# A fused attention and feed-forward kernel on one core: alternating K and Q transposes, finer loads for batch 0, a halved last tile, and paired scores from batch 1

## The chip, the core and the metric

The kernel runs on one core of a Trainium2 chip. The metric is the device time of one execution in microseconds (us), taken outside the profiler. The span in a profile is about 1.7 us shorter, because it begins at the first profiled instruction. Engines are named as in the profile: PE is the matrix engine (TensorE), PEld its weight loads, DVE VectorE, ACT ScalarE, POOL GpSimd, SP the engine that issues most DMAs, with q added for a sequencer.

Before the change the median was 360.2 us (359.94 to 360.87, 4 runs).

## The reference

Eight batches of gated attention (8 heads, 576 positions, head size 64) feed a gated feed-forward layer (width 512, hidden 1536).

```python
scores = q @ k.T / 8                                    # per batch and head
bias   = -(cum[:, None] - cum[None, :])                 # cum = cumsum(max(s, 0))
attn   = softmax(where(causal, -1e9, scores + minimum(bias, 0)))
x      = (attn @ v), heads joined                       # 4608 x 512
xn     = x / sqrt(mean(x * x) + 1e-6) * rms_g
out    = (silu(xn @ w_gate) * (xn @ w_val)) @ w_out     # 4608 x 512, float32
```

## The kernel before

The kernel records all operations with estimated durations. A list scheduler then fixes the order on each engine, and each operation is emitted in that order. `R.after(a, b)` is only an order for that scheduler. On the chip it holds where both stand on the same engine; between two engines only data dependencies make one wait.

The output tokens are worked off in nine chunks of 512. For each chunk, PE does the gate and value products (FFN1), then the output product (FFN2). The attention of the next batch is woven in between. The attention of batch 0 has to come first, and so it stands alone at the start.

These parts matter here (cuts are marked):

```python
def prep_transpose(b, which, hp, key, eng):             # K or Q of one head pair
    ...
    mms(0.6, [(t[64*j:64*j+64, c, :], raw[b][p0:p0+KP, 2*hp+j, c, :], ident_bf[...],
               c == 0, c == KC-1, True) for c in range(KC) for j in range(2)], key=key)
    ...                                                 # evicted by DVE (K) or ACT (Q)

def decay(key):                                         # DVE: max, then a scan of 64 x 576
    I("dve", "tensor_scalar", ..., out=s_all, in0=s_all, scalar1=0.0, op0=ALU.max)
    I("dve", "tensor_tensor_scan", ..., out=cum, data0=ones[...], data1=s_all, ...)
    ...

def att_out(b, tb, key):                                # scale a tile of rows, transpose it
    ...
    I("act", "activation", 0.5, out=x, in_=x, func=AF.Copy, scale=al[b % 2][:, 1, tb:tb+1])
    ...

def ffn2(c, key, step):                                 # O: 128 tokens x 512
    for tb in range(4):
        ...                                             # 12 matmuls of 512 columns
        I("act", "activation", 0.6, out=o, in_=O, func=AF.Copy, scale=0.5)
        I("sp", "dma_start", ..., out=out[t0+tb*128 : t0+(tb+1)*128, :], in_=o)

NTWO = 2                                                # paired scores from this batch on
WL = (0, 6, 12)                                         # gate and value weights in two pieces
...
for i in range(2):
    for w in range(2):
        load_runs(0, w, 2*i, 2*i+2, -100+i)             # K, Q, two heads each
for w in range(2):
    load_runs(0, w, 4, 8, -98)                          # K, Q, the other four heads
ident(ident_bf, -97)                                    # identity for the transposes, on POOL
ident(ident_F, -96)
load_rows(v_nat[0], v, 0, "pool", -94)
...
R.after(vops[2], norms[3])                              # v products of batch 0 on DVE
for o in wl[2:]:
    R.after(o, masks[0, HP-1])                          # second half of the weights
```

Of the kernel before, what the change touches and what calls it, by code (L numbers as in the profile page):

```python
# [75 lines left out]
class Plan:  # L76
# [58 lines left out]

    def schedule(self):
# [15 lines left out]
        def ready(o):  # L152
            t = 0.0
            for p, raw in o.preds.items():
                q = ops[p]
                if q.eng == o.eng and not q.dma:
                    t = max(t, q.done if raw and o.eng != "pe" else q.start)
                else:
                    t = max(t, q.done + self.HOP)
            return t  # L160
# [88 lines left out]
def kernel(  # L249
# [41 lines left out]
    NTWO = 2  # L291
# [138 lines left out]
    def prep_transpose(b, which, hp, key, eng):  # L430
        p0, dst = KP * which, (KT, QT)[which]
        t = lay(small_bank(), bf16, "p (c t) -> p c t", n=S, c=KC)
        mms(0.6, [(t[64 * j : 64 * j + 64, c, :], raw[b][p0 : p0 + KP, 2 * hp + j, c, :],
                   ident_bf[p0 : p0 + KP, p0 : p0 + KP],
                   c == 0, c == KC - 1, True) for c in range(KC) for j in range(2)], key=key)
        o = dst[b % 2][:, hp, 0:S].rearrange("p (t c) -> p t c", c=KC)
        i = t.rearrange("p c t -> p t c")
        if eng == "dve":
            I("dve", "tensor_copy", 0.68, key=key, out=o, in_=i)
        else:  # L440
            I("act", "activation", 0.57, key=key, out=o, in_=i, func=AF.Copy)
# [98 lines left out]
    masks = {}  # L540

    def unit_scores(b, us, keys, Es, cap):
# [11 lines left out]
        o = mms(0.1 + 0.32 * len(us), items, key=keys[0])  # L554
        for u, key in zip(us, keys):
            e = Es[u] = nxt("E", E)
            for j in range(2):
                I("act", "activation", 0.5, key=key, out=e[:, j], in_=banks_[u][j], func=AF.Exp,
                  scale=0.125)
            diag = e.rearrange("p j (c n) -> p (j c) n", n=128)[:, 0:8:2, :]  # L560
            masks[b, u] = I("pool", "affine_select", 0.59, key=key, out=diag, in_=diag,
              pattern=[[0, 4], [1, 128]], compare_op=ALU.is_ge, fill=0.0, base=0,
              channel_multiplier=-1)
            if u >= HP:
                last = e[:, :, 448:512]
                I("pool", "affine_select", 0.28, key=key, out=last, in_=last,
                  pattern=[[0, 2], [1, 64]], compare_op=ALU.is_ge, fill=0.0, base=0,
                  channel_multiplier=-1)
        return o

    def unit_av(b, u, key, Es):
# [10 lines left out]
        mms(0.2 if hf == 0 else 0.4,  # L582
# [20 lines left out]
    def att_alpha(b, t0, t1, key):  # L603
# [3 lines left out]
        I("pool", "tensor_tensor", 0.94, key=key, out=y, in0=m, in1=mhalf[:, 0 : t1 - t0],  # L607
          op=ALU.pow)

    def att_out(b, tb, key):  # L610
        x = x_blk[b % 2][:, tb, :]
        if b >= NPE:
# [7 lines left out]
        I("act", "activation", 0.5, key=key, out=x, in_=x, func=AF.Copy,  # L620
          scale=al[b % 2][:, 1, tb : tb + 1])
        p0 = 64 if tb == 4 else 0
        X = lay(small_bank(), bf16, "p (c t) -> p c t", n=DM, c=CC)
        mms(0.24, [(X[:, cc, :], x_blk[b % 2][:, tb, cc * 128 : (cc + 1) * 128], ident_bf,
# [6 lines left out]
    def attention(b, key, step, cap):  # L631
# [8 lines left out]
        for hf in range(2):  # L640
# [6 lines left out]
            att_alpha(b, tbs[0], tbs[-1] + 1, k2)  # L647
# [24 lines left out]
    def ffn2(c, key, step):  # L672
        t0 = c * DM
        for tb in range(4):
            O = bank("ffn", 6)
            for f in range(0, FB, 2):
                mms(0.432, [(O, Hs[:, fb, tb * 128 : (tb + 1) * 128], wout_sb[:, fb, :],
                             fb == 0, fb == FB - 1, False) for fb in (f, f + 1)],
                    key=key + step * (tb * FB + f))
            o = nxt("osb", osb)  # L680
            I("act", "activation", 0.6, key=key + step * (tb * FB + FB), out=o, in_=O,
              func=AF.Copy, scale=0.5)
            I("sp", "dma_start", 0.62, key=key, dma=0.75,
              out=out[t0 + tb * 128 : t0 + (tb + 1) * 128, :], in_=o)
# [3 lines left out]
    WL = (0, 6, 12)  # L688
# [11 lines left out]
    for i in range(2):  # L700
        for w in range(2):
            load_runs(0, w, 2 * i, 2 * i + 2, -100 + i)
# [4 lines left out]
    for w in range(2):  # L707
        load_runs(0, w, 4, 8, -98)
    ident(ident_bf, -97)
    ident(ident_F, -96)  # L710
    load_rows(v_nat[0], v, 0, "pool", -94)
# [11 lines left out]
    for hp in range(HP):  # L723
        prep_transpose(0, 0, hp, -80 + hp, "dve")
        prep_transpose(0, 1, hp, -80 + hp, "act")
# [6 lines left out]
    R.after(vops[2], norms[3])  # L732
    for o in wl[2:]:
        R.after(o, masks[0, HP - 1])
    raw_norm(0, 20)
    for w in range(2):
        for h in (0, 4):
            R.after(load_runs(1, w, h, h + 4, -45), masks[0, 2 * HP - 1])
    load_rows(v_nat[1 % len(v_nat)], v, 1, "pool", -44)
    for i in range(2):  # L740
        load_w(2, 6 * i, 6 * i + 6, -40)
    gl = I("sp", "dma_start", 0.5, key=30, dma=2.0, out=gB,
           in_=moe_rms_g.unsqueeze(0).to_broadcast([128, DM]))
    for c in range(NCH):
# [5 lines left out]
        if b < B:  # L750
            if b < NRUN:
                for hp in range(HP):
                    prep_transpose(b, 0, hp, K + hp, "dve")
                    prep_transpose(b, 1, hp, K + hp, "act")
            else:
                prep_cast(b, K - 14)
# [193 lines left out]
```

## Time and profile before

| What | Value | View |
|---|---|---|
| time | 360.2 us | timed runs |
| PE busy | 339.0 of 358.9 us | page, part 1 |
| first FFN1 matmul | 25.2 us | timeline |
| last PE work, end of span | 352.8, 358.9 us | timeline |

The page's part 1 gives busy microseconds, the share of the span and the instructions. Part 4 gives the shares of the chain that ended last.

```profile
PE 339.0 (94%) x2934; PEld 206.7 (58%) x2934; DVE 247.0 (69%) x486; ACT 231.6 (65%) x469; POOL 126.5 (35%) x211
...
PE 78%; DMA 9%; POOL 6%; DVE 3%; issue 1%; ACT 1%; DVEq 0%; POOLq 0%; ACTq 0%
```

PE is the bound. The run is the time until the first FFN1 matmul, plus the PE work after it, plus a tail. The next fence is the list of what PE waited for (what waited, what released it, total us, times, longest).

```profile
PE psa L376 <- POOL ident_bf masks.py:199: 5.8, 1, 5.8
PE psd L378 <- DVE vwa L361: 2.5, 1, 2.5
...
PE pse L376 <- ACT x_blka L361: 0.5, 1, 0.5
PE psg L376 <- ACT x_blka L361: 0.4, 1, 0.4
...
PE psh L376 <- ACT x_blka L361: 0.2, 1, 0.2
```

The first wait is for the identity. The 2.5 us are attention-times-V products (AV) of the second half of batch 0, which need a v product. The waits for `x_blka` are for scaled rows.

Next are PE's weight loads in batch 1, where PE is never idle. Each line with `k_nat` is one group of K or Q transposes.

```profile
38.54 0.65 PEld L376 LDWEIGHTS <-k_nat 64*64 64x64 bf16 x36 [0.21 <-issue]
...
40.20 0.55 PEld L376 LDWEIGHTS <-k_nat 64*64 64x64 bf16 x36 [0.21 <-issue]
...
41.77 0.36 PEld L376 LDWEIGHTS <-k_nat 64*64 64x64 bf16 x18 [0.21 <-issue]
```

A group of 18 that stands alone occupies PE for 0.40 us, counted from its start to the start of the next work. Two groups side by side take 0.69 and 0.59.

The tail, as the timeline and the list of DMA issues of that window have it (the last column of the issue is the time to landing):

```profile
352.92 0.60 ACT L361 ACTIVATE osbc<-psb 128x512 f32<-128x512 f32 x1 [2.04 <-PE psb L378]
353.54 0.33 SPq L361 DMA_DIRECT2D out_dram<-osbc  x1
```

```profile
out_dram<-osbc SPq DMA_DIRECT2D x1, 256.0 KB, 3.5
```

### The profile page before, as it was taken

To read this page: it belongs to the slowest core of one execution; us is meant where nothing else is said; L and a number is where in the kernel's file an instruction comes from. 1 tells how busy PE (TensorE), PEld (TensorE's weight loads), DVE (VectorE), ACT (ScalarE), POOL (GpSimd) and SP (SyncE) were. 2 spreads that over 40 slices of the span, in tenths; PEclk is the share of its full clock that TensorE was granted. 3 is DMA by queue.
4 is the path that set the end of the run, shared out by engine and by line. 5 is a ranking of instruction groups with operands and counts; after the bars stand their busy time and mean duration, and the time that the engine had idled before them with its cause. 6 is when DMAs were issued, how large, how long until landed. Compare 5 with 4: busy or idle time off the path is not lost.

```text
span 358.9 us, 7827 instructions
## 1 busy us (share of the span) xinstructions
PE 339.0 (94%) x2934; PEld 206.7 (58%) x2934; DVE 247.0 (69%) x486; ACT 231.6 (65%) x469; POOL 126.5 (35%) x211
## 2 busy tenths in 40 slices
PE   2969999999999999999999999999999999999993
PEld 2657776698668875888444554445445444444441
DVE  6586965798848992899467967995489538707820
ACT  3858998597678857877677568775876433233311
POOL 8987273301480375117502650357124100000000
PEclk9989999999999999999999999999999999999998
DMA  7999999999999899869978989995801150020011
GB/s 118 211 226 208 216 204 204 172 213 195 203 154 231 170 144 215 189 123 170 207 154 163 182 175 178 164 187 104 177 9 31 55 102 1 1 89 29 0 62 64
DMA packets 138357, 51.14 MB, mean 142 GB/s; under 512 B 127300, under 2 KB 132936, under 8 KB 138312
## 3 DMA queue, kind: packets, MB, share of 16 engines
q1 hardware_dynamic: 131688, 41.13, 60.9%
q0 software_dynamic: 6624, 9.44, 14.4%
q8 instruction: 25, 0.41, 0.5%
q14 instruction: 20, 0.16, 0.2%
HBM read 38.16 MB, written 9.44 MB: 133 GB/s over the span
## 4 chain that ended last, share of the span: by engine, by line
PE 78%; DMA 9%; POOL 6%; DVE 3%; issue 1%; ACT 1%; DVEq 0%; POOLq 0%; ACTq 0%
PE pse L378 12%; PE psa L378 10%; PE psh L378 10%; PE psb L378 10%; PE psf L378 9%; PE psd L378 9%; PE psc L378 9%; PE psg L378 8%; DMA wv_sb<-in_moe_w_val_dram 5%; DMA v_nata<-in_v_dram 4%; POOL v_nata L361 2%; POOL q_nat L361 1%; ACT sq_scr L361 1%; DVE Hs L361 1%; POOL Ee L361 1%
## 5 line engine op out<-in xcount | busy, mean ns | idle before, releaser
L378 PEld LDWEIGHTS <-wv_sb 128*128 128x128 bf16 x624 | 59.9, 98 | 32.9 <-issue 1.3
L378 PEld LDWEIGHTS <-wg_sb 128*128 128x128 bf16 x624 | 59.2, 98 | 30.7 <-issue 0.8
L378 PEld LDWEIGHTS <-Hs 128*128 128x128 bf16 x432 | 41.0, 98 | 45.6
L361 POOL TENSOR_SCALAR_AFFINE_SELECT Ea<-Ea 128x512 bf16<-128x512 bf16 x8 | 5.6, 699 | 61.6 <-ACT Ea L361 61.6
L361 POOL TENSOR_TENSOR vwb<-v_nata,wT 128x512 bf16<-128x512 f32 (+1 forms) x20 | 20.6, 1049 | 6.8 <-DMA v_nata<-in_v_dram 6.8
L378 PE MATMUL pse<-wout_sb,Hs 128*128 128x512 bf16 x96 | 22.5, 379 | 0.0
L378 PE MATMUL psf<-xnT,wv_sb 128*128 128x256 bf16 (+1 forms) x116 | 20.7, 313 | 0.0
L361 ACT ACTIVATE sq_scr<-x_blka 128x512 bf16<-128x512 bf16 x19 | 12.0, 630 | 12.0 <-DVE x_blka L361 11.6
L378 PE MATMUL psc<-xnT,wg_sb 128*128 128x256 bf16 (+1 forms) x104 | 18.8, 316 | 0.0
L361 DVE SCALAR_TENSOR_TENSOR x_blkb<-x_blkb,alb,gB 128x512 bf16<-128x512 bf16 x15 | 11.0, 779 | 10.8 <-POOL alb L361 10.7
L361 ACT ACTIVATE sq_scr<-x_blkb 128x512 bf16<-128x512 bf16 x20 | 12.6, 629 | 7.8 <-DVE x_blkb L361 7.3
L378 PE MATMUL psh<-wout_sb,Hs 128*128 128x512 bf16 x72 | 17.2, 379 | 0.0
L378 PE MATMUL psa<-wout_sb,Hs 128*128 128x512 bf16 x72 | 17.0, 379 | 0.0
L378 PE MATMUL psb<-xnT,wv_sb 128*128 128x256 bf16 (+1 forms) x100 | 16.5, 302 | 0.2 <-DVE u_sbc L361 0.2
L378 PE MATMUL psd<-xnT,wg_sb 128*128 128x256 bf16 (+1 forms) x88 | 16.5, 321 | 0.0
L361 ACT ACTIVATE sq_scr<-q_bf 128x1024 bf16<-128x1024 bf16 (+1 forms) x18 | 16.4, 912 | 0.1
L361 ACT ACTIVATE sq_scr<-k_bf 128x1024 bf16<-128x1024 bf16 (+1 forms) x18 | 16.3, 908 | 0.0
L361 DVE CAST q_bf<-q_nat 128x512 bf16<-128x512 f32 (+1 forms) x30 | 15.3, 510 | 0.9 <-ACT sq_scr L361 0.9
L378 PE MATMUL pse<-xnT,wg_sb 128*128 128x256 bf16 (+1 forms) x92 | 15.5, 305 | 0.0
L378 PE MATMUL psa<-xnT,wg_sb 128*128 128x256 bf16 (+1 forms) x84 | 15.5, 318 | 0.0
L361 POOL TENSOR_TENSOR vwa<-v_nata,wT 128x512 bf16<-128x512 f32 (+1 forms) x15 | 15.1, 1039 | 0.0
L361 DVE CAST k_bf<-k_nat 128x512 bf16<-128x512 f32 (+1 forms) x30 | 13.7, 456 | 0.0
(464 smaller groups left out, 850.4 us busy)
## 6 DMA issues: line engine op xcount, KB each, us to landing
v_nata<-in_v_dram SPq DMA_DIRECT2D x24, 256.0 KB, 5.3
k_nat<-in_k_dram SPq DMA_DIRECT2D x24, 256.0 KB, 3.6
q_nat<-in_q_dram SPq DMA_DIRECT2D x24, 256.0 KB, 4.5
out_dram<-osba SPq DMA_DIRECT2D x12, 256.0 KB, 2.4
out_dram<-osbb SPq DMA_DIRECT2D x12, 256.0 KB, 2.5
out_dram<-osbc SPq DMA_DIRECT2D x12, 256.0 KB, 2.4
v_nata<-in_v_dram POOLq DMA_DIRECT2D x8, 256.0 KB, 10.4
wg_sb<-in_moe_w_gate_dram POOLq DMA_DIRECT2D x2, 768.0 KB, 12.2
```

The source lines that it names most:

```text
L361: o = R.add(eng, us, lambda: f(**{n: real(a) for n, a in kw.items()}), outs, ins, key=key, lat=LAT[eng], kind=kind, dma=dma, name=outs[0]. ...
L378: nc.tensor.matmul(out, lhsT=lhsT, rhs=rhs, start=st, stop=sp)
```

## The change

The intent is to shorten the start (earlier identity, loads in finer pieces and in a fixed order, v products and one scaling moved), to let the K and Q transposes of a head pair share PE (they use different 64-row halves of it), to pay the cost of entering and leaving the scores less often in batch 1, and to shorten the last eviction and store. The durations that the scheduler assumes were also re-measured, which re-orders the later batches a little.

```diff
-    NTWO = 2
+    NTWO = 1
...
-    def prep_transpose(b, which, hp, key, eng):
-        p0, dst = KP * which, (KT, QT)[which]
-        t = lay(small_bank(), bf16, "p (c t) -> p c t", n=S, c=KC)
-        mms(0.6, [( ... ) for c in range(KC) for j in range(2)], key=key)
+    def prep_transpose(b, hp, key):
+        t = [lay(bank("kq", 4), bf16, "p (c t) -> p c t", n=S, c=KC) for w in range(2)]
+        mms(0.52, [( ... ) for c in range(KC) for j in range(2) for w in range(2)], key=key)
...
-        I("act", "activation", 0.5, key=key, out=x, in_=x, func=AF.Copy, scale=...)
+        if b == 0 and tb == 1:
+            I("dve", "tensor_scalar", 0.3, key=key, out=x, in0=x, scalar1=..., op0=ALU.mult)
+        else:
+            I("act", "activation", 0.72, key=key, out=x, in_=x, func=AF.Copy, scale=...)
...
+            nh = 2 if c == NCH - 1 and tb == 3 else 1       # ffn2: last tile in halves
+            ...                                             # matmuls, eviction, store per half
-    WL = (0, 6, 12)
+    WL = (0, 2, 6, 12)
...
-    for w in range(2):
-        load_runs(0, w, 4, 8, -98)
-    ident(ident_bf, -97)
+    loads += [load_runs(0, w, 2 * i, 2 * i + 2, -98) for i in (2, 3) for w in range(2)]
+    ident(ident_bf, -98.5)                                  # now before these four loads
...
-    R.after(vops[2], norms[3])
-    for o in wl[2:]:
+    for o in vops[2:]:
+        R.after(o, norms[3])
+    for o in loads[15:]:                                    # weights from the 2nd piece on
         R.after(o, masks[0, HP - 1])
+    for o in wl[4:]:                                        # 3rd piece
+        R.after(o, alphas[0, 0])
+    R.order(*loads)
```

Besides this, the masks and the power of batch 0's first half got priority on POOL, and batch 0's transposes of x got their own group of banks.

More of the change, by code (lines that the diff above doesn't have):

```diff
@@ L134, in after, with order @@
             o.preds.setdefault(p.n, False)
+    def order(self, *ops):
+        for p, o in zip(ops, ops[1:]):
+            o.preds.setdefault(p.n, None)
     def schedule(self):
@@ L155, in ready @@
                 q = ops[p]
-                if q.eng == o.eng and not q.dma:
+                if raw is None:
+                    t = max(t, q.start)
+                elif q.eng == o.eng and not q.dma:
                     t = max(t, q.done if raw and o.eng != "pe" else q.start)
@@ L427, in load_w @@
                  in_=src[:, lo:hi].rearrange("(cc p) f -> p cc f", p=128))
-    def prep_transpose(b, which, hp, key, eng):
-        p0, dst = KP * which, (KT, QT)[which]
-        t = lay(small_bank(), bf16, "p (c t) -> p c t", n=S, c=KC)
-        mms(0.6, [(t[64 * j : 64 * j + 64, c, :], raw[b][p0 : p0 + KP, 2 * hp + j, c, :],
-                   ident_bf[p0 : p0 + KP, p0 : p0 + KP],
-                   c == 0, c == KC - 1, True) for c in range(KC) for j in range(2)], key=key)
-        o = dst[b % 2][:, hp, 0:S].rearrange("p (t c) -> p t c", c=KC)
-        i = t.rearrange("p c t -> p t c")
-        if eng == "dve":
-            I("dve", "tensor_copy", 0.68, key=key, out=o, in_=i)
-        else:
-            I("act", "activation", 0.57, key=key, out=o, in_=i, func=AF.Copy)
+    def prep_transpose(b, hp, key):
+        t = [lay(bank("kq", 4), bf16, "p (c t) -> p c t", n=S, c=KC) for w in range(2)]
+        mms(0.52, [(t[w][64 * j : 64 * j + 64, c, :], raw[b][KP * w : KP * w + KP, 2 * hp + j, c, :],
+                    ident_bf[KP * w : KP * w + KP, KP * w : KP * w + KP],
+                    c == 0, c == KC - 1, True)
+                   for c in range(KC) for j in range(2) for w in range(2)], key=key)
+        for w, dst in enumerate((KT, QT)):
+            o = dst[b % 2][:, hp, 0:S].rearrange("p (t c) -> p t c", c=KC)
+            i = t[w].rearrange("p c t -> p t c")
+            if w == 0:
+                I("dve", "tensor_copy", 0.68, key=key, out=o, in_=i)
+            else:
+                I("act", "activation", 0.57, key=key, out=o, in_=i, func=AF.Copy)
     def prep_cast(b, key):
@@ L538 @@
               ((2, 0, 256, 512), (3, 256, 384, 576), (4, 448, 512, 576)))
-    masks = {}
+    masks, alphas = {}, {}
     def unit_scores(b, us, keys, Es, cap):
@@ L553, in unit_scores @@
                                   QT[b % 2][rs, hp, q0:q1], i == 0, i == len(gs) - 1, False))
-        o = mms(0.1 + 0.32 * len(us), items, key=keys[0])
+        o = mms(0.21 + 0.22 * len(us), items, key=keys[0])
         for u, key in zip(us, keys):
@@ L560, in unit_scores @@
             diag = e.rearrange("p j (c n) -> p (j c) n", n=128)[:, 0:8:2, :]
-            masks[b, u] = I("pool", "affine_select", 0.59, key=key, out=diag, in_=diag,
+            masks[b, u] = I("pool", "affine_select", 0.59, key=-200 if b == 0 and u < HP else key, out=diag, in_=diag,
               pattern=[[0, 4], [1, 128]], compare_op=ALU.is_ge, fill=0.0, base=0,
@@ L581, in unit_av @@
         AV = lay(small_bank(), fp32, "p (j t d) -> p j t d", n=2 * nq * 65, j=2, t=nq)
-        mms(0.2 if hf == 0 else 0.4,
+        mms(0.19 if hf == 0 else 0.36,
             [(AV[:, j, qb - q0, :], e[:, j, c0 : c0 + 128], vw[b % 2][:, kb, 2 * hp + j, :],
@@ L606, in att_alpha @@
           scalar1=1.0 / DM, scalar2=1e-6, op0=ALU.mult, op1=ALU.add)
-        I("pool", "tensor_tensor", 0.94, key=key, out=y, in0=m, in1=mhalf[:, 0 : t1 - t0],
+        alphas[b, t0] = I("pool", "tensor_tensor", 0.94, key=key, out=y, in0=m, in1=mhalf[:, 0 : t1 - t0],
           op=ALU.pow)
@@ L619, in att_out @@
             return
-        I("act", "activation", 0.5, key=key, out=x, in_=x, func=AF.Copy,
-          scale=al[b % 2][:, 1, tb : tb + 1])
+        if b == 0 and tb == 1:
+            I("dve", "tensor_scalar", 0.3, key=key, out=x, in0=x,
+              scalar1=al[b % 2][:, 1, tb : tb + 1], scalar2=None, op0=ALU.mult)
+        else:
+            I("act", "activation", 0.72, key=key, out=x, in_=x, func=AF.Copy,
+              scale=al[b % 2][:, 1, tb : tb + 1])
         p0 = 64 if tb == 4 else 0
-        X = lay(small_bank(), bf16, "p (c t) -> p c t", n=DM, c=CC)
-        mms(0.24, [(X[:, cc, :], x_blk[b % 2][:, tb, cc * 128 : (cc + 1) * 128], ident_bf,
+        X = lay(bank("xt", 2) if b == 0 else small_bank(), bf16, "p (c t) -> p c t", n=DM, c=CC)
+        mms(0.22, [(X[:, cc, :], x_blk[b % 2][:, tb, cc * 128 : (cc + 1) * 128], ident_bf,
                     cc == 0, cc == CC - 1, True) for cc in range(CC)], key=key)
@@ L646, in attention @@
                 att_square(b, tb, k2, "dve" if b == 0 and tb == 1 else "act")
-            att_alpha(b, tbs[0], tbs[-1] + 1, k2)
+            att_alpha(b, tbs[0], tbs[-1] + 1, -200 if b == 0 and hf == 0 else k2)
             for tb in tbs:
@@ L674, in ffn2 @@
         for tb in range(4):
-            O = bank("ffn", 6)
-            for f in range(0, FB, 2):
-                mms(0.432, [(O, Hs[:, fb, tb * 128 : (tb + 1) * 128], wout_sb[:, fb, :],
-                             fb == 0, fb == FB - 1, False) for fb in (f, f + 1)],
-                    key=key + step * (tb * FB + f))
-            o = nxt("osb", osb)
-            I("act", "activation", 0.6, key=key + step * (tb * FB + FB), out=o, in_=O,
-              func=AF.Copy, scale=0.5)
-            I("sp", "dma_start", 0.62, key=key, dma=0.75,
-              out=out[t0 + tb * 128 : t0 + (tb + 1) * 128, :], in_=o)
+            rows = slice(t0 + tb * 128, t0 + (tb + 1) * 128)
+            nh = 2 if c == NCH - 1 and tb == 3 else 1
+            w = DM // nh
+            for h in range(nh):
+                cols = slice(h * w, h * w + w)
+                O = bank("ffn", 6)
+                for f in range(0, FB, 2):
+                    mms(0.432 / nh, [(O[:, 0:w], Hs[:, fb, tb * 128 : (tb + 1) * 128],
+                                      wout_sb[:, fb, cols], fb == 0, fb == FB - 1, False)
+                                     for fb in (f, f + 1)],
+                        key=key + step * (tb * FB + h * FB / nh + f / nh))
+                o = nxt("osb", osb)
+                I("act", "activation", 0.6 / nh, key=key + step * (tb * FB + FB), out=o[:, 0:w],
+                  in_=O[:, 0:w], func=AF.Copy, scale=0.5)
+                I("sp", "dma_start", 0.62, key=key, dma=0.75, out=out[rows, cols], in_=o[:, 0:w])
     whole = [(0, DM, fb) for fb in range(FB)]
     halves = [(o, 256, fb) for o in (0, 256) for fb in range(0, FB, 2)]
-    WL = (0, 6, 12)
+    WL = (0, 2, 6, 12)
     first = [(o, 256, fb) for lo, hi in zip(WL, WL[1:]) for o in (0, 256)
@@ L699 @@
     fill("dve", w_row[:, S : NB * 128], 0.0, 0.1, key=-100)
-    for i in range(2):
-        for w in range(2):
-            load_runs(0, w, 2 * i, 2 * i + 2, -100 + i)
+    loads = [load_runs(0, w, 2 * i, 2 * i + 2, -100) for i in range(2) for w in range(2)]
     def ident(t, key):
         R.add("pool", 0.5, lambda: make_identity(nc, t), [t], [], key=key, lat=0.06).n_pool = 2
-    for w in range(2):
-        load_runs(0, w, 4, 8, -98)
-    ident(ident_bf, -97)
+    loads += [load_runs(0, w, 2 * i, 2 * i + 2, -98) for i in (2, 3) for w in range(2)]
+    ident(ident_bf, -98.5)
     ident(ident_F, -96)
-    load_rows(v_nat[0], v, 0, "pool", -94)
+    loads += load_rows(v_nat[0], v, 0, "pool", -94)
     wl = []
@@ L723 @@
     for hp in range(HP):
-        prep_transpose(0, 0, hp, -80 + hp, "dve")
-        prep_transpose(0, 1, hp, -80 + hp, "act")
+        prep_transpose(0, hp, -80 + hp)
     gp_ = bank("g", 1)
@@ L731 @@
     norms = attention(0, -78, 3, 4)
-    R.after(vops[2], norms[3])
-    for o in wl[2:]:
-        R.after(o, masks[0, HP - 1])
-    raw_norm(0, 20)
-    for w in range(2):
-        for h in (0, 4):
-            R.after(load_runs(1, w, h, h + 4, -45), masks[0, 2 * HP - 1])
-    load_rows(v_nat[1 % len(v_nat)], v, 1, "pool", -44)
-    for i in range(2):
-        load_w(2, 6 * i, 6 * i + 6, -40)
+    for o in vops[2:]:
+        R.after(o, norms[3])
+    raw_norm(0, 20)
+    kq1 = [load_runs(1, w, h, h + 4, -45) for h in (0, 4) for w in range(2)]
+    v1 = load_rows(v_nat[1 % len(v_nat)], v, 1, "pool", -44)
+    w2 = [load_w(2, 6 * i, 6 * i + 6, -40) for i in range(2)]
+    loads += wl + kq1 + w2[:1] + v1 + w2[1:]
+    for o in loads[15:]:
+        R.after(o, masks[0, HP - 1])
+    for o in wl[4:]:
+        R.after(o, alphas[0, 0])
+    for o in kq1 + v1 + w2:
+        R.after(o, masks[0, 2 * HP - 1])
+    R.order(*loads)
     gl = I("sp", "dma_start", 0.5, key=30, dma=2.0, out=gB,
@@ L752 @@
                 for hp in range(HP):
-                    prep_transpose(b, 0, hp, K + hp, "dve")
-                    prep_transpose(b, 1, hp, K + hp, "act")
+                    prep_transpose(b, hp, K + hp)
             else:
```

## The prediction

> **What bounds it now.** TensorE. The page gives PE 339.0 of 358.9 us busy (94%). The chain that ended last is 78% PE, 9% DMA, 6% POOL. By the windows, from 30 us to the tail the PE is busy over 96% of the time, so the run is: the time until the first feed-forward matmul, plus all PE work after it, plus a tail. The timeline has that matmul at 25.2 us. Before it the PE is busy for only about half the time. After it the list of PE waits holds about 3 us, of which 1.1 us is at 31 us, for the scaled rows of batch 0's later tiles. The last PE work ends at 352.8; 6 us of eviction, store and ending follow.
>
> **Start.** The chain: fourth normalisation ends 20.1, square 20.9, the power on POOL 22.05, two scalings of 0.66 us one after the other on ACT 23.4, transposes, two xnT copies, first feed-forward matmul 25.2. The change:
> - puts the three later v products (0.68 us each on DVE) after the fourth normalisation; two stood in front of the third and fourth: about 1 us;
> - puts one scaling on DVE: 0.3 to 0.6 us;
> - has the bf16 identity made after four load issues instead of six (0.65 us each). First transposes could start near 5.3 instead of 5.8, and the first exponentials move from 10.3 towards 8. But the third and fourth head pairs still wait for loads (DMA share above 1 from 5 us on), and ACT is dense from 9.8 to 19.5; most of this won't reach the end of the chain.
> - Two AV groups (0.33 us each) move behind the first feed-forward group: 0.7 us is displaced, not saved. The first feed-forward weights need only 2/12 loaded.
>
> First feed-forward matmul: near 23.7 (22.5 to 24.8); net of the displaced work, about 0.9 us gained. The clock fell to 0.50 in 22.5 to 25 us after a 2.5 us PE wait; the Trainium skill, TensorE: Matmul & The Clock Gate ("What's actually happening"), has the clock halved after an idle window of about 3.4 us. A denser start should shorten this dip: 0.3 us.
>
> **Later PE work.** Batch 1's 144 transposes take 3.08 us, start to start: 0.40 us per 18 alone, but 0.59 in the pair where K's and Q's 64-row tiles alternate. The Trainium skill, TensorEngine Tiling (Array Packing), "Key Properties", says such tiles run in parallel; the 0.59 agrees. Four pairs at 0.55: 0.9 us gained. Single scores in batch 1 pay about 0.09 us on entering and 0.09 on leaving (a pair in batch 2 takes 0.55, a single one 0.32): four pairings, 0.5 us. The 1.1 us wait at 31 us mostly goes, because other groups stand before those transposes: 0.6 us.
>
> **Tail.** The last eviction is 0.60 us for 512 columns; half of it, and half the store behind it, give 0.5 us.
>
> **Sum.** 0.9 + 0.3 + 0.9 + 0.5 + 0.6 + 0.5 = 3.7 us. The later batches are only re-ordered: either sign, about 1 us. Predicted 356.5 us, 8 in 10 between 353.0 and 359.0. Faster by over 2% 0.11, within 2% 0.87, slower 0.02.
>
> **What would show it.** First feed-forward matmul near 23.7; PE busy near 337; transposes near 0.55 us a pair; last eviction near 0.35 us; PE idle before 30 us smaller, clock dip shorter.
>
> **What would make it wrong.** Weights in three pieces, the later ones issued only after masks and the power on POOL, could arrive late, so that the PE waits between 25 and 35 us (slower). The earlier exponentials could carry through to the first feed-forward matmul, 21 to 22 us (then 353). A re-ordered middle could lose or gain a microsecond or two at batch boundaries.

## More of the kernel before

The timeline of POOL and DVE at the start (start us, duration us, engine, operation) shows how the identity is made: a memset, then a select.

```profile
3.52 0.67 DVE L361 TENSOR_SCALAR s_all<-s_all 64x576 f32<-64x576 f32 x1 [0.85 <-DMA s_all<-in_s_dram]
...
4.22 1.35 DVE L361 TENSOR_TENSOR_SCAN s_all<-ones,s_all 64x576 f32<-64x576 f32 x1
...
5.09 0.28 POOL masks.py:197 MEMSET ident_bf<- 128x128 bf16 x1
...
5.45 0.29 POOL masks.py:199 TENSOR_SCALAR_AFFINE_SELECT ident_bf<-ident_bf 128x128 bf16<-128x128 bf16 x1
```

The memset and the select come after six load issues, at 5.09 and 5.45 us, and DVE's scan has just ended when the select is done. Transposes begin at 5.79.

## The result, and the profile after

The changed kernel has a median of 358.24 us (357.7 to 358.41, 4 runs) against 360.2. The ratio is 0.994, with a 95% interval of 0.9923 to 0.9958: same, at 2%. A ratio is the mean time of one kernel's fast runs over that of the other's of the same rounds, so it isn't quite the ratio of the medians quoted.

The page after, parts 1 and 4:

```profile
PE 336.5 (95%) x2946; PEld 205.6 (58%) x2946; DVE 248.3 (70%) x487; ACT 230.6 (65%) x469; POOL 132.9 (37%) x215
...
PE 86%; DVE 5%; POOL 3%; DMA 2%; issue 1%; ACT 1%; DVEq 0%; ACTq 0%; POOLq 0%
```

To see where the time went, the run is cut at PE events that both traces have: the first FFN1 matmul, and the start of the last FFN2 matmul of the first, the sixth and the ninth output chunk. PE does the same work before each of these chunk marks in both kernels. Because runs of one program scatter, the kernel before was profiled twice (the second is an experiment below).

| Stage, us | Before | Before, second profile | Changed |
|---|---|---|---|
| to the first FFN1 matmul | 25.2 | 24.8 | 25.9 |
| from there to the end of chunk 1 | 43.2 | 43.4 | 40.9 |
| to the end of chunk 6 | 185.6 | 185.1 | 185.4 |
| to the end of chunk 9 | 98.5 | 98.5 | 99.4 |
| to the end of the span | 6.5 | 6.2 | 4.4 |
| span | 358.9 | 357.9 | 356.0 |

So the start became no faster, the first chunk gained 2.4 us, the later batches lost 0.9 us, and the tail gained about 2 us. Whether the start became slower isn't shown: up to the first FFN1 matmul four profiles have the order of the kernel before, with 24.8, 25.2, 25.5 and 25.7 us there, and two have that of the changed kernel, with 24.7 and 25.9 (the others are the experiments `tail_only`, `pe_halves` and `ntwo2` below). The profiled span fell by 2.9 us against the one profile and by 1.9 against the other. The medians fell by 2.0.

The waits of PE after, to be compared with those before:

```profile
PE psa L382 <- POOL ident_bf masks.py:199: 5.7, 1, 5.7
PE psd L384 <- DVE vwa L367: 2.2, 1, 2.2
PE psg L384 <- DVE vwa L367: 2.1, 3, 1.4
...
PE psd L384 <- DVE xnT L367: 0.3, 1, 0.3
```

The identity is only 0.1 us earlier, PE now waits for v products once for 2.2 us and three more times for 2.1 us together, and the waits at 31 us are gone. The timeline of the same stretch of the start:

```profile
3.73 0.45 DVE L367 TENSOR_SCALAR s_all<-s_all 64x576 f32<-64x576 f32 x1 [1.06 <-DMA s_all<-in_s_dram]
3.85 0.47 POOL masks.py:197 MEMSET ident_bf<- 128x128 bf16 x1
4.21 1.35 DVE L367 TENSOR_TENSOR_SCAN s_all<-ones,s_all 64x576 f32<-64x576 f32 x1
4.39 1.26 POOL masks.py:199 TENSOR_SCALAR_AFFINE_SELECT ident_bf<-ident_bf 128x128 bf16<-128x128 bf16 x1
...
5.61 0.61 POOL L367 DMA_DIRECT2D q_nat<-in_k_dram  x1
```

The memset and the select now begin at 3.85 and 4.39 us, but the select lasts 1.26 us in place of 0.29 and ends at 5.65, just after DVE's scan. The load behind it is issued at 5.61, where before the corresponding load was issued at 3.87.

The transposes of batch 1 (PE's weight loads, two head pairs in each line):

```profile
39.48 0.74 PEld L382 LDWEIGHTS <-k_nat 64*64 64x64 bf16 x72 [0.21 <-issue]
...
45.43 0.74 PEld L382 LDWEIGHTS <-k_nat 64*64 64x64 bf16 x72 [0.21 <-issue]
```

Each group of 72 takes 0.79 us, from its start to that of the next work. And the tail:

```profile
351.99 0.38 ACT L367 ACTIVATE osba<-psb 128x256 f32<-128x256 f32 x1 [0.93 <-PE psb L384]
352.40 0.33 SPq L367 DMA_DIRECT2D out_dram<-osba  x1
```

```profile
out_dram<-osba SPq DMA_DIRECT2D x1, 128.0 KB, 1.8
```

### The profile page after: what moved, and what is told of

Its sections match the earlier page's. It is cut to its first block, busy times and chain, and to the rows that moved or that the text cites. A ratio compares the mean times of both kernels' runs of the same rounds, so it can differ in the third digit from the quotient of the medians.

```text
span 356.0 us, 7884 instructions
## 1 busy us (share of the span) xinstructions
PE 336.5 (95%) x2946; PEld 205.6 (58%) x2946; DVE 248.3 (70%) x487; ACT 230.6 (65%) x469; POOL 132.9 (37%) x215
## 4 chain that ended last, share of the span: by engine, by line
PE 86%; DVE 5%; POOL 3%; DMA 2%; issue 1%; ACT 1%; DVEq 0%; ACTq 0%; POOLq 0%
PE pse L384 12%; PE psd L384 11%; PE psh L384 11%; PE psb L384 11%; PE psf L384 11%; PE psg L384 10%; PE psc L384 9%; PE psa L384 9%; DMA v_nata<-in_v_dram 2%; POOL q_nat L367 1%; DVE x_blka L367 1%; ACT sq_scr L367 1%; POOL vwb L367 1%; DVE vwa L367 1%; DVE u_sbb L367 1%
## 5 line engine op out<-in xcount | busy, mean ns | idle before, releaser
L384 PEld LDWEIGHTS <-Hs 128*128 128x128 bf16 x444 | 41.5, 98 | 42.2
L384 PE MATMUL psf<-wout_sb,Hs 128*128 128x512 bf16 x84 | 19.9, 379 | 0.0
L384 PE MATMUL psd<-xnT,wg_sb 128*128 128x256 bf16 (+1 forms) x104 | 18.1, 312 | 0.3 <-DVE xnT L367 0.3
L384 PE MATMUL pse<-wout_sb,Hs 128*128 128x512 bf16 x72 | 17.8, 379 | 0.0
L384 PE MATMUL psh<-xnT,wv_sb 128*128 128x256 bf16 (+1 forms) x104 | 17.6, 306 | 0.2 <-DVE u_sbb L367 0.2
L384 PE MATMUL psd<-wout_sb,Hs 128*128 128x512 bf16 x72 | 17.2, 379 | 0.0
L384 PE MATMUL psf<-xnT,wv_sb 128*128 128x256 bf16 (+1 forms) x96 | 16.5, 308 | 0.0
L384 PE MATMUL psb<-xnT,wg_sb 128*128 128x256 bf16 (+1 forms) x96 | 16.5, 308 | 0.0
L384 PE MATMUL pse<-xnT,wv_sb 128*128 128x256 bf16 (+1 forms) x92 | 16.5, 314 | 0.0
L384 PE MATMUL psa<-xnT,wv_sb 128*128 128x256 bf16 (+1 forms) x92 | 15.5, 305 | 0.0
L384 PE MATMUL psg<-xnT,wv_sb 128*128 128x256 bf16 (+1 forms) x88 | 15.5, 311 | 0.0
```

The lines of the kernel that those rows point to most:

```text
L384: nc.tensor.matmul(out, lhsT=lhsT, rhs=rhs, start=st, stop=sp)
```

## The experiments

All but one of the kernels were timed in five rounds against the kernel before on the same chip, and profiled. Differences of less than about 1 us between medians of different calls mean little here. Most readings therefore come from the traces.

### The last tile alone (`tail_only`)

The kernel before, with `ffn2` of the changed kernel and nothing else.

```diff
+            nh = 2 if c == NCH - 1 and tb == 3 else 1
+            ...                       # the last tile's matmuls, eviction and store in halves
```

> The kernel before with one part of the change: the last output tile computed, evicted and stored in halves. Prediction's theory (a smaller eviction and a smaller store, 0.5 us): 359.7 us, ratio to before 0.9985; the last eviction near 0.38 us. Theory from the two profiles (from the end of the last eviction to the end of the span it took 5.4 us in before and 3.6 in the changed kernel, mostly because the last store landed 3.1 us after its issue in one and 1.4 in the other): about 1.5 to 2 us, 358.5 us, ratio 0.995, and the same short last store in this profile. Rival: the long last store of before was chance (an instruction fetch lay across it), and this kernel's gain is 0.5 us at most in the medians.

Measured: 358.46 us (356.98 to 359.19), ratio 0.9945 (0.9921 to 0.9969). The last eviction took 0.38 us, and the list of DMA issues of the tail has:

```profile
out_dram<-osbc SPq DMA_DIRECT2D x1, 128.0 KB, 3.0
out_dram<-osba SPq DMA_DIRECT2D x1, 128.0 KB, 2.0
```

The last store lands 2.0 us after its issue, against 3.5 before. This part of the change alone gives about as much as the whole change. The prediction's 0.5 us was too small by a factor of three or four.

### The kernel before, a second time

An identical program, one run (state unknown).

> The kernel before, once more, for a second profile of the same program. If the long last store (3.1 us from issue to its last byte, with an instruction fetch across it) belongs to the program, it is here again; if it was chance, the store takes 1.7 us as the earlier ones at the end do, and the span is about 357.5. The first feed-forward matmul tells how far it scatters between runs of one program: 25.2 us within 0.5.

Measured: 359.71 us, first FFN1 matmul at 24.8 us. The line of the tail is:

```profile
out_dram<-osbc SPq DMA_DIRECT2D x1, 256.0 KB, 3.3
```

So the long last store belongs to the program. In both profiles of before, the trace's DMA records show fetches of instructions that overlap it: one of 16 KB from 354.28 to 355.29 us and two of 8 KB, while the store's data moved from 354.37 to 356.62. The four stores of the same size ahead of the last one had their last byte 1.66 to 1.97 us after the issue. The last one needed 3.08, and 2.82 in the second profile.

### The last tile's matmuls in halves, eviction and store whole (`pe_halves`)

```diff
-                mms(0.432, [(O, ..., wout_sb[:, fb, :], fb == 0, fb == FB - 1, False) ...
+            for h in range(nh):       # nh = 2 for the last tile, O is one bank
+                mms(0.432 / nh, [(O[:, cols], ..., wout_sb[:, fb, cols], ...
```

> The kernel before, with only the matmuls of the last output tile in two halves (24 more weight loads and matmuls in all); one eviction and one store, as before. If the long last store of before came from instruction fetches that fall into it, and the halves in the changed kernel gain by moving the TensorE program's fetches, then the store here takes about 1.7 us in place of 3.1 and the time falls by about 1.2 us: 359.0, ratio 0.9965. If the size of eviction and store is what counts, the store stays near 3 us and the time is that of before within 0.3 us, ratio 1.000.

Measured: 359.51 us (358.92 to 360.15), ratio 0.9983 (0.9967 to 0.9998). The line of the tail:

```profile
out_dram<-osbc SPq DMA_DIRECT2D x1, 256.0 KB, 2.5
```

The extra PE instructions moved the 16 KB fetch away from the store (it now lies at 352.48 to 353.40 and 355.57 to 356.53). The store's last byte came 2.20 us after the issue in place of 3.08. Two 8 KB fetches remain across it. The expected 1.7 us was not reached, and the ratio moved by 0.17% in place of 0.35%. Where the fetches fall is thus a part of the tail's gain, about 0.6 us in time. How the rest divides between the smaller store, the smaller eviction (0.2 us) and the other fetches was not separated.

### Transposes not alternating

The changed kernel with the order of matmuls inside each group changed; the order on all other engines is identical.

```diff
-                   for c in range(KC) for j in range(2) for w in range(2)], key=key)
+                   for w in range(2) for c in range(KC) for j in range(2)], key=key)
```

> The changed kernel with the K and Q transposes of a pair not alternating: first 18 of K, then 18 of Q, in the same matmul group; nothing else differs on any engine. If alternating is worth what batch 1 shows (two pairs in 0.79 us, against 0.6 to 0.8 us for one pair before), the four pairs of batch 1 take 2.4 to 3.0 us in place of 1.57 and the total rises by 1 to 1.5 us over the changed kernel, ratio to before about 0.998. If the transposes of batch 0 count as well, up to 2 us, ratio 0.9995. Rival: the PE isn't what bounds these stages and the total stays within 0.3 us of the changed kernel, ratio 0.994.

Measured: 357.81 us (357.52 to 358.49), ratio 0.9936 (0.9918 to 0.9954), so no slower than the changed kernel. The weight loads of batch 1's transposes:

```profile
38.41 0.93 PEld L382 LDWEIGHTS <-k_nat 64*64 64x64 bf16 x72 [0.21 <-issue]
...
44.55 0.93 PEld L382 LDWEIGHTS <-k_nat 64*64 64x64 bf16 x72 [0.21 <-issue]
```

Two head pairs take 0.97 us from start to next start, against 0.79 when they alternate. Four pairs therefore lose 0.36 us, not the 1 to 1.5 expected. So 1.1 us of the gain (3.08 to 1.57 us for the four pairs) doesn't need the alternation. The starts of the single matmuls in the traces say where it comes from. Two transposes of one 64-row half start together every 31.6 ns, and a stay costs about 0.12 us beyond that: 18 transposes take 0.40 us, 36 of K alone 0.69. Where 18 of K stand next to 18 of Q, the starts of the two groups overlap by about 0.1 us even without alternation: 36 take 0.59, and 72 with three such neighbours 0.97. The kernel before had six stays with one such overlap. Here there are two stays with three overlaps each, because the change puts K and Q of a pair into one group, and the scheduler put two pairs side by side. An estimate from these numbers is 0.5 us for four stays fewer and 0.5 us for five overlaps more. Another 0.2 us is one group of 18 that took 0.60 us in the kernel before. The Trainium skill, "TensorEngine Tiling (Array Packing)", "Key Properties", says that a change of the tiling mode drains the engine, and these numbers agree with a fixed cost per stay. In batch 0, at half clock, alternation shortened a pair from 0.92 to between 0.63 and 0.70 us where no wait lay in it, but there PE waits for loads and for ACT anyway: the first FFN1 matmul came at 25.0 us here.

### Identity after all eight loads

```diff
-    ident(ident_bf, -98.5)
+    ident(ident_bf, -97)
```

> The changed kernel with the bf16 identity built after all eight K and Q loads of batch 0, not after four. Theory: the early identity was not ready earlier (5.65 us against 5.74 before, its select took 1.26 us while a VectorE scan ran) and held back the four later loads and all of V by 1.7 to 2.3 us, so that the first AV group waited 2.2 us for V. Then here V is first issued near 7.2 us in place of 8.5, the first AV wait falls below 1 us, the first feed-forward matmul comes 1 to 2 us earlier than 25.9, and the total is 356.5 to 357.5 us, ratio to before about 0.990. Rival: eight smaller loads in place of six are what delays V (then V is as late, the wait stays near 2 us and so does the time), or the first transposes, now 1 us later, take the gain back.

Measured: 359.21 us (357.25 to 361.65), ratio 0.9964 (0.9928 to 1.0001). The select took 0.29 us again and V was first issued at 7.26 us, as expected. But the first FFN1 matmul stayed at 25.7 us: the transposes began at 6.8, and the first AV wait was 1.4 us, with 1.1 for ACT ahead of it. The later batches were re-ordered as well and the third chunk took 2.1 us longer. This is a miss: it shows that the load issues were held up, not that giving them back this way helps.

### DVE's scan held until the identity is ready

One tiny copy on DVE, which reads the identity and writes a cell that is overwritten later, stands in front of the scan.

```diff
     def decay(key):
+        I("dve", "tensor_copy", 0.06, key=key, out=half, in_=ident_bf[0:BH, 0:1])
```

> The changed kernel with one tiny VectorE copy that reads the identity ahead of the VectorE scan, so that the scan can't start before the identity is ready. Theory: the identity's select on GpSimd was slowed by the scan [...]. Then the select takes about 0.3 us in place of 1.26, the identity is ready near 4.7 us, the later loads and V are issued 0.9 us earlier than in the changed kernel, the first AV wait falls from 2.2 to about 1.2 us, the first feed-forward matmul comes 0.5 to 1 us earlier; total 357.3 to 357.8, ratio 0.992. Rival: the first use of select pays a fixed start-up, or GpSimd works off the descriptors of its loads first; then the select still ends near 5.6 us and nothing moves.

Measured: 357.64 us (356.9 to 359.12), ratio 0.9938 (0.9912 to 0.9963). The timeline of the start:

```profile
3.86 0.46 POOL masks.py:197 MEMSET ident_bf<- 128x128 bf16 x1
4.40 0.29 POOL masks.py:199 TENSOR_SCALAR_AFFINE_SELECT ident_bf<-ident_bf 128x128 bf16<-128x128 bf16 x1
4.64 0.61 POOL L367 DMA_DIRECT2D q_nat<-in_k_dram  x1
...
4.72 0.15 DVE L367 CAST half<-ident_bf 64x1 f32<-64x1 bf16 x1 [0.54 <-POOL ident_bf masks.py:199]
...
4.79 1.34 DVE L367 TENSOR_TENSOR_SCAN s_all<-ones,s_all 64x576 f32<-64x576 f32 x1
```

The select takes 0.29 us, the identity is ready at 4.69, and the next load is issued at 4.64 in place of 5.61. The rivals (a fixed start-up, or descriptors to be worked off) would have left the select where it was; they are out. The Trainium skill, "GPSIMD Engine Reference", "1. Specifications", says that GpSimd's SBUF interfaces are shared with VectorE, with contention for instructions with two SBUF inputs or in a two-port mode. The scan has two SBUF inputs, and the trace agrees: 1.26 us beside it, 0.29 without. The memset, which reads nothing, took 0.28 us in the middle of the scan in the kernel before. That the scan lengthens the select is shown; that it does so through this interface is the page's reading and wasn't tested apart.

The first FFN1 matmul came at 23.8 us, 2.2 earlier than in the changed kernel and close to the predicted 23.7. Not all of the 2.2 us belongs to the collision, since the second profile of this program (next experiment) has 24.3 and the second one of the changed start 24.7. A steadier mark is the start of the first AV group that needs the late v product. It lies at 16.0, 16.2 and 17.2 us in the three profiles with the early identity beside the scan, and at 15.1 to 16.5 in the six with the held scan; by the means, the collision costs 0.9 us there. In time, neither this kernel nor the next can be told from the changed one. And the end of chunk 1 came only 0.5 us earlier. PE's waits tell one half of it:

```profile
PE psg L384 <- DVE vwa L367: 1.8, 2, 1.4
...
PE psg L384 <- DMA wv_sb<-in_moe_w_val_dram: 1.2, 1, 1.2
```

FFN1 now waits 1.2 us, at 34 us, for value weights. The other half is the clock. Matmuls of 256 columns start 0.21 us apart at first and 0.11 later; this kernel had eight slow ones after its first FFN1 matmul, which cost 0.8 us by those intervals, and the changed kernel had five (0.5 us). The AV work behind them took 0.99 us here and 0.73 there.

### Two v products no longer deferred: an edit without effect

The held scan, with the old line for the v products. Only DVE's order was meant to differ.

```diff
-    for o in vops[2:]:
-        R.after(o, norms[3])
+    R.after(vops[2], norms[3])
```

> The kernel with the held scan, with two of the three later v products of batch 0 no longer held behind the fourth normalisation (as before); nothing but VectorE's order differs. The prediction's step: the deferral gains 1 us at the first feed-forward matmul; then it comes 0.7 to 1.3 us later here than 23.8. Rival from the trace: the deferred products stand between the square and the second scaling, and an AV group that waits for them (2.1 us) stands in front of the transposes on TensorE; then those waits fall below 1 us here and the first feed-forward matmul is at 23.3 us or earlier. Total within 0.7 us of the held scan either way.

Measured: 357.59 us (357.07 to 359.92), ratio 0.9949 (0.9923 to 0.9976). The first FFN1 matmul came at 24.3 us, 0.6 later than in the held scan, and PE still waited 2.4 us for v products. But this is no test of the deferral. In the two traces, the instructions of every engine stand in the same order by operation and tile, and three v products follow the square in both (from 19.42 and 19.74 us): the scheduler left them where they were without the rule. So it is a second profile of the held scan. It shows that the first FFN1 matmul scatters by 0.6 us between profiles of one program. The wait of 1.2 us for weights isn't in this profile at all; here AV groups wait 0.9 us for masks instead, and chunk 1 ends at 66.4 us, against 66.2. So where no wait for weights is seen in the next experiments, that may be chance too. What the deferral is worth stays untested.

### Weights issued one step earlier

The held scan, with the gates for the second and third piece of the weights moved up.

```diff
     for o in loads[15:]:
-        R.after(o, masks[0, HP - 1])
+        R.after(o, masks[0, 1])
     for o in wl[4:]:
-        R.after(o, alphas[0, 0])
+        R.after(o, masks[0, HP - 1])
```

> The kernel with the held scan, and the weights' second and third pieces issued one step earlier each (after the second and the fourth mask, in place of the fourth mask and the power). Theory: with the identity out of the way the first feed-forward matmul comes at 23.8 us, but the DMA engines were left short (132 GB/s in 15 to 20 us against 194 before), so that the feed-forward part waited 1.2 us for value weights at 34 us and most of the gain was lost. Here 15 to 20 us moves over 160 GB/s, the wait at 34 us is gone, the first feed-forward matmul is at 23.3 to 24.3 us; total 356.3 to 357.0, ratio 0.990, against 0.9938 for the held scan alone. Rival: the small pieces and not the gates cost the rate, or the masks behind the earlier issues are late; then no gain over the held scan.

Measured: 358.2 us (357.78 to 358.86), ratio 0.9949 (0.9935 to 0.9964). The wait for weights is gone and the first chunk ended at 65.0 us, the earliest of all. But the scheduler put the transposes of x in front of an AV group, PE waited 3.0 us for scaled rows, and the next three chunks took 1.8 us longer than in the changed kernel (0.7 of it is AV work moved there). No gain in time.

### Weights in two pieces, 6/12 and 6/12

```diff
-    WL = (0, 2, 6, 12)
+    WL = (0, 6, 12)
```

(on top of the held scan)

> The kernel with the held scan, and the gate and value weights in two pieces again (6/12 and 6/12) in place of three (2/12, 4/12, 6/12). In 15 to 20 us the DMA engines were busy in every kernel, but moved 132 to 173 GB/s in those with three pieces and 194 to 197 in before: theory, the narrow first pieces (rows of 512 bytes) cost the rate, and the later weights come late for it. Here 15 to 20 us moves 185 GB/s or more, no wait for value weights at 34 us, the first feed-forward matmul is at 23.5 to 24.5 us, and from it to the end of the first output chunk it takes 41.0 us or less (42.5 in the held scan); total about 356.6 us, ratio 0.990. Rival: the first piece, now three times as large, is late itself (first feed-forward matmul after 25 us), or the re-ordered later batches take the gain; then 0.994 as before.

Measured: 362.36 us (361.57 to 363.42), ratio 1.0002 (0.9964 to 1.004), a miss in time. The DMA rate between 15 and 20 us rose to 187 GB/s as expected and no wait for weights is left. The first FFN1 matmul came at 25.5 us, though, and from chunk 1 to chunk 4 it took 118.0 us against 111.7 in the changed kernel, with PE waits for masks and scaled rows of batch 1 between 67 and 79 us. A re-ordered middle can thus cost 6 us.

### Weights in two pieces, 4/12 and 8/12, run twice

```diff
-    WL = (0, 2, 6, 12)
+    WL = (0, 4, 12)
```

(on top of the held scan)

> The same with pieces of 4/12 and 8/12 (rows of 1024 and 2048 bytes). Small-piece theory: a rate between the two, about 175 GB/s in 15 to 20 us, and the first feed-forward matmul at 23.5 to 24.3 us. The second piece is larger and lands later, so a wait for weights between 30 and 36 us of up to 1 us may stay. Total between 356.6 and 357.6.

Measured: 357.41 us (356.07 to 357.64), ratio 0.9866 (0.9831 to 0.9902). The kernel before scattered from 360.63 to 364.69 on that chip, and so it was run again:

> The kernel with the held scan and weight pieces of 4/12 and 8/12, once more, because the chip of its first run gave scattered times for the kernel before (360.6 to 364.7). If the gain is real, its median is 356.5 to 357.5 us and the ratio to before 0.988 to 0.992, below the changed kernel's 0.994 and the held scan's 0.9938; in the profile the first feed-forward matmul is at 24.4 us within 0.5, and there is no wait for weights. If the first ratio, 0.9866, came from the chip alone, it is 0.993 or above here.

Measured: 357.44 us (356.62 to 358.59), ratio 0.9917 (0.9885 to 0.9949). There is no wait for weights. It beats the kernel before. Its second interval overlaps that of the changed kernel, so that it beats the changed kernel too is likely but not shown.

The windows view, 15 to 20 us, of before, the held scan and this one (stretch, its length, busy us and instructions of each engine, clock, mean DMA share, GB/s):

```profile
15.00:20.00 5.00, 3.98 (x47) 2.54 (x45) 3.38 (x11) 4.48 (x9) 5.00 (x8) 1.00 1.16 194
```

```profile
15.00:20.00 5.00, 3.48 (x43) 2.29 (x42) 3.78 (x12) 4.90 (x12) 4.87 (x8) 1.00 1.05 132
```

```profile
15.00:20.00 5.00, 3.44 (x42) 2.29 (x42) 3.67 (x12) 3.90 (x10) 4.11 (x7) 1.00 1.17 177
```

The 132 GB/s of the held scan are partly chance: its second profile moved 161, at a busy share of 1.29. The rate for a given busy share is steadier. Divided by the share, the seven profiles with rows of 512 bytes in the first piece moved 118 to 134 GB/s in this stretch, the two with 1024 bytes 151 and 154, and the five with 1536 bytes (two pieces of 6/12) 164 to 171. So the narrow rows cost rate, as expected. Moving the gates raised the rate to 173 by a larger busy share (1.34), at the same 129 GB/s for a share of 1.

The two profiles of this one program also show how large the luck is. These are its first FFN1 groups, first run and then second (PE's timeline):

```profile
24.38 1.87 PE L384 MATMUL psd<-xnT,wg_sb 128*128 128x256 bf16 x8 [0.78 <-DVE xnT L367]
...
27.32 1.04 PE L384 MATMUL pse<-xnT,wv_sb 128*128 128x256 bf16 x8
28.19 1.04 PE L384 MATMUL psa<-xnT,wg_sb 128*128 128x256 bf16 x8
```

```profile
24.84 1.86 PE L384 MATMUL psd<-xnT,wg_sb 128*128 128x256 bf16 x8 [0.78 <-DVE xnT L367]
...
27.83 1.90 PE L384 MATMUL pse<-xnT,wv_sb 128*128 128x256 bf16 x8
29.52 1.56 PE L384 MATMUL psa<-xnT,wg_sb 128*128 128x256 bf16 x8
30.93 1.04 PE L384 MATMUL psb<-xnT,wv_sb 128*128 128x256 bf16 x8
```

A group of eight takes about 1.9 us at the low clock and 1.04 at the full one. The first run was at full clock from 27 us on, the second from about 30. This alone makes 1.4 us, and the first chunk differs by just that (41.5 and 42.9 us).

### Single scores in batch 1 (`ntwo2`)

```diff
-    NTWO = 1
+    NTWO = 2
```

(on the changed kernel)

> The changed kernel with single scores in batch 1, as before; paired ones from batch 2 on. The scores of batch 1 took 2.83 us before and 2.41 after, start to start. If pairing is what saved it, batch 1's scores are back near 2.8 us here, and from the first feed-forward matmul to the end of the first output chunk it takes about 41.3 us in place of 40.9; total within 0.7 us of the changed kernel, set more by how the later batches fall than by this.

Measured: 359.09 us (357.23 to 361.95), ratio 0.9927 (0.9882 to 0.9973). Batch 1's scores took 3.35 us with waits and 2.66 without, against 2.41 paired. In the four profiles with the order of the kernel before they took 2.62 to 2.83 without waits, so the pairing saves 0.2 to 0.4 us on PE. From the first FFN1 matmul to the end of chunk 1 it took 42.0 us in place of 40.9; the rest of that difference lies in AV work (3.7 us in place of 2.9) and waits. In time the kernel can't be told from the changed one on that scattered chip.

## Why the prediction was right, and where it was not

The time was predicted as 356.5 us with a range of 353.0 to 359.0, within 2%. Measured were 358.24 us, within the range and within 2%. The direction and the place of the bound were right. Of the sum, several terms were wrong and partly cancelled, so that a total inside the range was in part luck: the start gained nothing where 0.9 us net was expected, and the tail gained 1.4 to 1.6 us more than expected.

| Term | Predicted, us | Measured, us |
|---|---|---|
| first FFN1 matmul | 25.2 to 23.7 | from 24.8 to 25.7 (four profiles) to 24.7 and 25.9 (two) |
| AV work displaced behind it | +0.7 | +0.7 (27.29 to 28.02 us) |
| half-clock loss | -0.3 | about +0.3 to +0.5 |
| batch 1's transposes | -0.9 | -1.5 |
| batch 1's paired scores | -0.5 | -0.2 to -0.4 |
| waits at 31 us | -0.6 | -0.6 |
| later batches | 0, either sign by 1 | +0.9 |
| tail | -0.5 | -1.9 to -2.1 |

The rows for the first chunk (AV work, half clock, transposes, scores, waits) add up to a gain of 1.1 to 1.5 us, and the stage gained 2.4. PE's start-to-start times hold the rest: the AV work that both kernels have there took 2.2 us in place of 2.9 (before, groups of 6 stood alone), and waits of AV groups fell by 0.4 us. The prediction has neither, and the first scatters: AV work with the changed kernel's order took up to 0.75 us more in other profiles.

- **"First feed-forward matmul: near 23.7": wrong.** It was to come 1.5 us earlier through the v products and the scaling; of the identity, the prediction itself said that "most of this won't reach the end of the chain". One cost was missing. The early identity ran beside the scan and was ready at 5.65 us, so that the transposes began at 5.7 and not at 5.3. It held back four K and Q loads and all of V, the first AV group waited 2.2 us for it, and ACT, whose exponentials wait for PE, stood still meanwhile. Holding the scan took about 0.9 us of this away, by the start of that AV group. The expected gain failed too: from the end of the fourth normalisation to the first FFN1 matmul it took 5.1 us before, 5.2 in the changed kernel, and 5.0 and 5.4 in the two profiles of the held scan. That one of these met 23.8 is therefore partly luck. The first exponentials did move from 10.3 to 7.9 us, as predicted.
- **The v products, "about 1 us": not tested.** They were taken out from in front of two normalisations, and three of them (1.9 us on DVE) then stood between the square and the scaling on DVE. An AV group that waits for them stands in front of the transposes of x. In the held scan the fourth normalisation ended at 18.8 us in place of 20.1; how much of that the deferral gave was not separated.
- **One scaling on DVE, "0.3 to 0.6 us": not seen.** It took 0.76 us on DVE in the changed kernel, about what ACT takes (0.72), and waited there behind the v products. In the held scan it took 0.35 us once and 0.75 the other time, for a reason that was not looked into.
- **"A denser start should shorten this dip": wrong.** The first FFN1 group ran at half speed in the changed kernel (1.53 us in place of 1.04). Over the traces the loss after the first FFN1 matmul ranged from 0 to 2 us, and from 0 to 0.9 over the four profiles with the order of the kernel before, so that the 0.3 to 0.5 us of the table are within chance. The Trainium skill, "TensorE: Matmul & The Clock Gate", "What's actually happening", describes a free-running window of about 3.4 us, so the moment of warming depends on where it falls; the two runs of one program that differ by 1.4 us agree.
- **Transposes, "four pairs at 0.55": right mechanism, size too small.** A pair took 0.39 us. K and Q side by side in their two row halves gave about 0.9 us by the estimate above, as predicted (0.5 by overlap without alternation, 0.36 by alternation). The fewer stays, about 0.5 us, had been left out.
- **Scores, "four pairings, 0.5 us": right in kind,** 0.2 to 0.4 measured.
- **The wait at 31 us, "mostly goes": right**, though its size had been added up wrongly: 1.1 us was read, but 0.5 of it lay before the first FFN1 matmul.
- **Tail, "give 0.5 us": mis-sized.** The eviction shrank by 0.2 us as predicted. The store shrank by 1.5 to 1.7 us. Part of this, about 0.6 us by the experiment above, is that a fetch of the program's last instructions no longer lies across it; the rest was not divided.
- **Weights that "could arrive late"** was named as a risk. In the changed kernel it did not show, because FFN1 itself began late. It appeared as a wait of 1.2 us in one of the two profiles of the held scan.

What stays open: what the deferral of the v products is worth, how the tail's gain divides beyond the part that the fetches have, and why the order of the later batches costs more. Of the 0.9 us lost there, 0.5 are two waits for DVE (one AV group, one FFN1 group), 0.3 are AV matmuls that took longer, and 0.14 are the halved last tile itself, which costs the same in `tail_only`.

## What to carry to other kernels

Before work is moved to an earlier time on one engine, look at what the engines that share a port or a queue with it are doing at that time; the profile shows this as the same instruction with a longer duration. An early gain only counts if the next supplier is early too: of the 2.2 us at the first FFN1 matmul, 0.5 were left at the end of chunk 1. When a large fixed cost sits in short stays (64-row matmuls, tails), count the stays, and look at one more profile of the same program before a microsecond is explained. And before an experiment is read, check in its trace that the edit changed the order that it was meant to change.

## What the Trainium skill lacked or had wrong

- "TensorEngine Tiling (Array Packing)" names the drain at a change of mode but no cost: about 0.12 us for each stay of 64x64 transposes at full clock, from 0.40 us for 18 and 0.69 for 36 in one row half, with two starting every 31.6 ns.
- "Runtime: NRT & Kernel Launch" doesn't say that fetches of instructions can lengthen a store: 3.08 and 2.82 us with fetches of 16 KB and 8 KB across it, 2.20 with the 16 KB one moved away, 1.66 to 1.97 for the stores ahead of it.
- No page says that a clock column tells nothing before the throttle's first record: in the held scan, whose first record is at 25.98 us, it shows 1.00 in 20 to 25 us, and the 256-column matmuls from 23.76 us on start 0.21 us apart, as against 0.11 after that record.
